# Decode attention over two KV caches: the V slots, the row length of A's V loads, and one softmax and one PV burst per K tile

## The chip, the cores and the metric

The kernel runs on one core of one Trainium2 chip. The core has five engines with instruction queues of their own: TensorE (PE), VectorE (DVE), ScalarE (ACT), GpSimd (POOL) and SyncE (SP). SP here does nothing but issue loads, in program order, on one load queue that 16 DMA engines work off. An engine waits for another through semaphores; an instruction that waits holds up all that stands behind it on its engine. The metric is the device time of one execution in microseconds (us): 830.06 is the median of three runs (829.58 to 830.49).

## The reference

Two independent attention blocks, A and B, each for a single query position, all in bf16:

```
q = x @ wq                      # x: 512 values, wq: 512 x 4096, 32 heads of 128
scores = q . k * 128**-0.5      # per head; every query head has its own K and V
p = softmax(scores)
o = p @ v                       # per head, 128 values
out = concat(o of 32 heads) @ wo   # wo: 4096 x 512
```

A attends to all 16384 positions of its cache, B to the last 4096 of its own. The result is A's 512 outputs followed by B's 512. K and V that must be read: A 32 heads x 16384 x 128 x 2 bytes twice, 268 MB; B 67 MB; the four weight matrices 16.8 MB; together 352 MB. There is one query per head, so every byte of K and V is used once.

## The kernel before, in words

**Tiles.** A "K tile" is 8 MB: 128 partitions with 256 positions of 128 values each. For A it holds a pair of heads (head h and 64 runs of 256 positions per head); for B two groups of four heads (4 heads x 32 runs of 128 positions per group, one group in each half of the tile). There are 20 K tiles, numbered T: 16 of A and 4 of B (T = 0, 7, 13 and 19). Each is worked on in two halves, u = 0 and 1, of `CH` = 128 positions per partition. To each K tile belongs a V tile of the same size and layout.

**Slots.** K tiles live in two slots of 64 KB per partition (`kring`). V lives in two slots of 32 KB per partition (`vring`), each a half V tile. The two wq matrices (4 MB each) start in the V slots. wo of A and the last half of V share the K slot that comes free at the end; wo of B takes a V slot.

**DVE: scores.** For each half tile: one product of K with q, 128x16384 (`scores_prod`, L194), four halving additions (`scores_tree`, L201), and a reduction to 128 scores per partition (L207). For A the two halves make one `Unit` (one softmax), for B each half is a unit of its own, with its own maximum.

**The softmax of a unit.** `unit_max` (L212, L214): DVE takes the maximum per partition, PE transposes it to one row. `max_all` (L219, L223, L226): DVE takes the maximum per head, spreads it, and PE turns it back into a column. `soft` (L231 to L242): ACT computes exp with its sum, and a masked copy of it per head (`pm`), so that heads in different partitions do not mix. `soft_sum` and `recip`: PE sums over partitions, DVE takes the reciprocal.

**PE: PV.** `pv` (L279) multiplies `pm` with V, four positions at a time: 32 matmuls of 128x512 per half V tile into one PSUM tile. `evict` (ACT, L295) scales it by the reciprocal, `columns` (PE L310, ACT L314) adds the four parts and turns it into columns of `O`. For the last K tile, `pv_columns` (L321) computes columns directly with 128 small matmuls per half.

**Order.** The whole program's order is written out by hand (`tc.manual_schedule()`): each engine runs its instructions in the order of these calls. In step T, u = 0, SP issues the first half of V(T-1), then K(T+1), and after the calls of PV the second half of V(T-1). The calls are:

```
            columns()
            scores_prod(T, u)
            if done is not None:
                max_all(done)
                soft(done)
                soft_sum(done)
            if u == 0 and T >= 1:
                if T >= 2:
                    pv(T - 2, 1)
                load_v(T - 1, 1)
                pv(T - 1, 0)
            nxt = scores_tree(T, u)
```

So one burst on PE is the second half of tile T-2 and the first half of tile T-1. A load is issued when the slot that it writes is free: K(T+1) when DVE is done with tile T-1, a V half when its slot's former PV is done.

**The end.** After the last K tile: the last softmax, the last PV half of tile 18, wo of B in five pieces (16, 8, 4, 2, 2 rows per partition, L145), `pv_columns` of the first half of tile 19, then for A `permute_o` (L331, L336), `project_out_columns` (L349, 128 small matmuls) and `store_out`; then `pv_columns` of the second half and the same three for B.

Of the kernel before, what the change touches and what calls it, by code (L numbers as in the profile page):

```python
# [25 lines left out]
def kernel(  # L26
# [26 lines left out]
    vring = ctx.enter_context(tc.tile_pool(name="vring", bufs=2))  # L53
# [10 lines left out]
    def vslot(name):  # L64
        return vring.tile([P, CH, DH], BF16, tag="vring", name=name)
# [58 lines left out]
    def load_v(T, u, dst=None):  # L124
        s, g = steps[T]
        V[T, u] = vslot("vt") if dst is None else dst
        if s is A:
            src = a_pair(A_v_cache, g)[:, u * CH : (u + 1) * CH, :].rearrange("p l d -> p (l d)")
        else:
            src = b_window(B_v_cache, 2 * g + u)  # L130
        nc.sync.dma_start(out=V[T, u][:, :, :].rearrange("p l d -> p (l d)"), in_=src)

    def load_wq(s):
        s.wq_t = vslot("wqt")
        nc.sync.dma_start(  # L135
            out=s.wq_t[:, :, :].rearrange("p a b -> p (a b)").rearrange("p (c f) -> p c f", c=KC),
            in_=s.wq.rearrange("(p c) f -> p c f", c=KC),
        )
# [24 lines left out]
    def project_q(s):  # L163
        wq = s.wq_t[:, :, :].rearrange("p a b -> p (a b)").rearrange(
            "p (c g h d) -> p c h g d", c=KC, h=s.nh, d=DH
        )
        for g in range(0, HQ // s.nh, 4):
            qp = ps_t.tile([P, 4, DH], F32, tag="tp", name="qp")
            n = KC * s.nh
            for k in range(n):  # L170
                c, j = divmod(k, s.nh)
                nc.tensor.matmul(  # L172
                    qp[:, :, :], lhsT=s.xb[:, j, c, :], rhs=wq[:, c, j, g : g + 4, :],
                    start=(k == 0), stop=(k == n - 1),
                )
            nc.scalar.copy(s.q[:, g : g + 4, :], qp[:, :, :])

    class Unit:
        def __init__(self, T, u):
            self.T = T  # L180
            self.s, g = steps[T]
            self.col = self.s.nh * g if self.s is A else self.s.nh * (2 * g + u)
            self.n = 2 * CH if self.s is A else CH
            self.rows = 4 * self.s.nh
            self.last = T == NT - 1
            self.sc = one.tile([P, 2 * CH], F32, tag="sc", name="sc")

# [8 lines left out]
    def scores_tree(T, u):  # L196
        s, g = steps[T]
        k = K[T][:, u * CH : (u + 1) * CH, :]
        w = DH // 2
        while w >= 8:  # L200
            nc.vector.tensor_tensor(out=k[:, :, 0:w], in0=k[:, :, 0:w], in1=k[:, :, w : 2 * w], op=ALU.add)  # L201
            w //= 2
        if s is B or u == 0:
            units[T, u] = Unit(T, u)
        un = units[T, u if s is B else 0]
        c0 = u * CH if s is A else 0
        nc.vector.tensor_reduce(out=un.sc[:, c0 : c0 + CH], in_=k[:, :, 0:8], axis=AX.X, op=ALU.add)  # L207
        return un if s is B or u == 1 else None

    def unit_max(un):  # L210
        m = small.tile([P, 1], F32, tag="m", name="m")
        nc.vector.tensor_reduce(out=m[:, :], in_=un.sc[:, 0 : un.n], axis=AX.X, op=ALU.max)  # L212
        un.sm = ps_m.tile([P, 512], F32, tag="sm", name="sm")
        nc.tensor.transpose(un.sm[0:1, 0:P], m[:, :], identf[:, :])  # L214

    def max_all(un):
        s = un.s
        M = small.tile([1, 4], F32, tag="M", name="M")
        nc.vector.tensor_reduce(  # L219
            out=M[:, 0 : s.nh], in_=by_head(s, un.sm[0:1, 0:P]), axis=AX.X, op=ALU.max  # L220
        )
        Mr = one.tile([1, P], F32, tag="Mr", name="Mr")
        nc.vector.tensor_copy(  # L223
            by_head(s, Mr[:, :]), M[:, 0 : s.nh].unsqueeze(2).broadcast_to([1, s.nh, P // s.nh])
        )
        nc.tensor.matmul(un.sm[:, 128:129], lhsT=Mr[:, :], rhs=one_f[:, :], start=True, stop=True)  # L226

    def soft(un):
        s = un.s
        bias = small.tile([P, 1], F32, tag="bias", name="bias")  # L230
        nc.scalar.activation(out=bias[:, :], in_=un.sm[:, 128:129], func=ACT.Copy, scale=-inv)  # L231
        p = one.tile([P, 2 * CH], BF16, tag="p", name="p")
        cs = small.tile([P, 1], F32, tag="cs", name="cs")
        nc.scalar.activation(  # L234
            out=p[:, 0 : un.n], in_=un.sc[:, 0 : un.n], func=ACT.Exp, scale=inv, bias=bias[:, :],
            accum_out=cs[:, :],
        )
        un.cs = cs
        pm = small.tile([P, 4 * CH], BF16, tag="pm", name="pm")
        un.pm = pm[:, 0 : un.n * s.nh].rearrange("p (i h c) -> p i h c", h=s.nh, c=4)  # L240
        for j in range(s.nh):
            nc.scalar.activation(  # L242
                out=un.pm[:, :, j, :], in_=p[:, 0 : un.n].rearrange("p (i c) -> p i c", c=4),
# [3 lines left out]
    def soft_sum(un):  # L247
        s, cs = un.s, un.cs
        if un.last:
            csm = small.tile([P, 4], F32, tag="csm", name="csm")  # L250
            nc.scalar.activation(out=csm[:, 0 : s.nh], in_=s.mask[:, :], func=ACT.Copy, scale=cs[:, :])
            nc.tensor.matmul(
                un.sm[:, 136 : 136 + s.nh], lhsT=ones_col[:, :].broadcast_to([P, P]), rhs=csm[:, 0 : s.nh],
                start=True, stop=True,
            )
        else:
            nc.tensor.matmul(  # L257
                un.sm[0 : un.rows, 136:137], lhsT=s.rows[:, :, :].rearrange("p a b -> p (a b)"), rhs=cs[:, :],
                start=True, stop=True,
            )  # L260

    def recip(un):
        un.r = small.tile([P, 4], F32, tag="r", name="r")
        if un.last:
            nc.vector.reciprocal(un.r[:, 0 : un.s.nh], un.sm[:, 136 : 136 + un.s.nh])
        else:
            nc.vector.reciprocal(un.r[0 : un.rows, 0:1], un.sm[0 : un.rows, 136:137])  # L267
# [3 lines left out]
    def pv(T, u):  # L271
        s = steps[T][0]
        un = units[T, u if s is B else 0]
        first, final = (True, True) if s is B else (u == 0, u == 1)
        if first:
            un.o = ps_o.tile([16, 512], F32, tag="o", name="o")
        i0 = u * CH // 4 if s is A else 0
        for i in range(CH // 4):
            nc.tensor.matmul(  # L279
                un.o[0 : un.rows, :],  # L280
                lhsT=un.pm[:, i0 + i, :, :].rearrange("p a b -> p (a b)"),
                rhs=V[T, u][:, 4 * i : 4 * i + 4, :],
                start=(first and i == 0),
                stop=(final and i == CH // 4 - 1),
            )
        if final:
            ready.append(un)
# [3 lines left out]
    def evict():  # L291
        while ready:
            un = ready.pop(0)
            un.osb = one.tile([16, 512], F32, tag="o4", name="o4")
            nc.scalar.activation(  # L295
                out=un.osb[0 : un.rows, :], in_=un.o[0 : un.rows, :], func=ACT.Copy,
                scale=un.r[0 : un.rows, 0:1],
            )
            evicted.append(un)
# [3 lines left out]
    def columns():  # L303
        while evicted:
            un = evicted.pop(0)
# [3 lines left out]
            for j in range(4):  # L309
                nc.tensor.matmul(  # L310
                    oc[:, 0 : s.nh], lhsT=un.osb[0:n, j * P : (j + 1) * P], rhs=sel[:, j, :],
                    start=(j == 0), stop=(j == 3),
                )
            nc.scalar.copy(s.O[:, un.col : un.col + s.nh], oc[:, 0 : s.nh])  # L314

    def pv_columns(T, u):
        un = units[T, u]
        s = un.s
        o = ps_o.tile([P, 4], F32, tag="o", name="ocol")
        for l in range(CH):  # L320
            nc.tensor.matmul(  # L321
                o[:, 0 : s.nh], lhsT=V[T, u][:, l, :], rhs=un.pm[:, l // 4, :, l % 4],
# [3 lines left out]
            out=s.O[:, un.col : un.col + s.nh], in0=o[:, 0 : s.nh], in1=un.r[:, 0 : s.nh], op=ALU.mult  # L326
# [51 lines left out]
    with tc.manual_schedule():  # L378
# [4 lines left out]
        load_wq(B)  # L383
        load_k(0, 0)
        load_wq(A)
# [17 lines left out]
        done = None  # L403
        for x in range(2 * NT):
            T, u = divmod(x, 2)
            if u == 0 and T >= 1:
                load_v(T - 1, 0)
# [3 lines left out]
            if x == 2 * NT - 2:  # L411
                W = kslot("wot")
                load_wo(A, W[:, 0:CH, :], (HQ,))
            if x == 2 * NT - 1:
                load_v(T, 0)
                load_v(T, 1, W[:, CH : 2 * CH, :])
            columns()
            scores_prod(T, u)
            if done is not None:
                max_all(done)  # L420
                soft(done)
                soft_sum(done)
            if u == 0 and T >= 1:
                if T >= 2:
                    pv(T - 2, 1)
                load_v(T - 1, 1)
                pv(T - 1, 0)
            nxt = scores_tree(T, u)
            if done is not None:
                recip(done)  # L430
            evict()
            done = nxt
            if done is not None:
                unit_max(done)
        columns()
        max_all(done)
        soft(done)
        pv(NT - 2, 1)
        load_wo(B, vslot("wot")[:, :, :], wo_pieces)
        soft_sum(done)  # L440
        recip(done)
        evict()
        pv_columns(NT - 1, 0)
        columns()
        permute_o(A)
        project_out_columns(A, (HQ,))
        store_out(A)
        pv_columns(NT - 1, 1)
# [33 lines left out]
```

## Time and profile before

| | |
|---|---|
| median of three runs | 830.06 us |
| the profiled execution's own time | 829.86 us |
| its span | 828.1 us |
| DVE busy | 761.4 us (92%) |
| PE busy | 387.3 us (47%) |
| ACT busy | 67.2 us (8%) |
| load queue of SP, share of the span of 16 DMA engines | 98.8% |
| read from HBM | 352.32 MB |
| last score of the last K tile (DVE, L207) ends | 791.4 us |
| last piece of B's wo is issued | 804.4 us |
| last output store is issued | 825.8 us |

The profile shows one execution, recorded by the hardware. A line of the timeline gives the start, the duration in us, the engine, the line of the program, the operation, what it writes and reads, the number of instructions merged into the line, and in brackets how long the engine sat idle before it and what ended that. "issue" means that nothing that the profile shows was waited for. A busy share is a mean over stages, and the slices (40 equal parts of the span) are read beside it: a digit of 9 is 90% or more. The granted clock of PE is 0.50 after idling, and 1.00 some microseconds into a burst.

### The profile page before, as it was taken

What the parts mean: (1) busy time and instruction counts of PE and PEld (TensorE: products, weight loads), DVE (VectorE), ACT (ScalarE), POOL (GpSimd) and SP (SyncE); (2) the same over time, 40 slices, a digit from 0 to 9 for tenths busy, and PEclk for the clock granted to TensorE, in tenths of its full rate; (3) what the DMA queues carried; (4) which work ended last, traced back from release to release, by engine and by line L of the source; (5) the groups of instructions that cost most, each with busy time, mean ns of one, the idle gap of its engine ahead of it and who ended that gap; (6) DMA issues with size and microseconds to landing.
All of it is one profiled execution on the core that took longest, in us unless ns stands there. A gap on an engine that the chain in (4) does not pass through costs nothing.

```text
span 828.1 us, 4994 instructions
## 1 busy us (share of the span) xinstructions
PE 387.3 (47%) x2100; PEld 171.3 (21%) x2100; DVE 761.4 (92%) x357; ACT 67.2 (8%) x195; POOL 0.7 (0%) x6
## 2 busy tenths in 40 slices
PE   3505061807173544637080826445362718081776
PEld 1201020303031212213030302122121203030335
DVE  1899999999999999999999999999999999999920
ACT  0111010101000001101010000011010101010110
POOL 0000000000000000000000000000000000000000
PEclk9766576859585868677685859586767767585975
DMA  9999999999999999999999999999999999999995
GB/s 380 431 431 431 428 453 423 449 416 436 431 427 431 431 440 423 439 423 455 412 450 416 452 412 432 442 423 445 419 443 418 441 421 444 424 432 432 430 430 240
DMA packets 10694, 352.64 MB, mean 426 GB/s; under 512 B 1456, under 2 KB 1456, under 8 KB 1840
## 3 DMA queue, kind: packets, MB, share of 16 engines
q1 hardware_dynamic: 10376, 352.33, 98.8%
q8 instruction: 16, 0.26, 0.1%
q10 hardware_dynamic: 296, 0.00, 0.0%
q14 instruction: 6, 0.05, 0.0%
HBM read 352.32 MB, written 0.00 MB: 425 GB/s over the span
## 4 chain that ended last, share of the span: by engine, by line
DVE 80%; DMA 15%; PE 3%; issue 1%; SPq 0%; ACT 0%; DVEq 0%
DVE kt L201 36%; DVE kt L194 36%; DMA kt<-in_A_k_cache_dram 10%; DVE sc L207 5%; DMA kt<-in_B_k_cache_dram 5%; PE o L279 1%; PE out_cols L349 1%; DVE m L212 1%; PE ocol L321 1%; DVE Mr L223 1%; DVE M L219 1%; DVE r L267 0%; SPq L135 0%; PE oc L310 0%; PE out_rows L367 0%
## 5 line engine op out<-in xcount | busy, mean ns | idle before, releaser
L201 DVE TENSOR_TENSOR kt<-kt 128x8192 bf16<-128x8192 bf16 (+3 forms) x160 | 344.9, 2156 | 4.7
L279 PE MATMUL o<-vt,pm 128*8 128x512 bf16 (+1 forms) x1216 | 306.7, 419 | 1.2 <-DMA vt<-in_A_v_cache_dram 1.2
L194 DVE TENSOR_TENSOR kt<-kt,qA 128x16384 bf16<-128x16384 bf16 x32 | 277.5, 8673 | 3.1 <-DMA kt<-in_A_k_cache_dram 3.1
L279 PEld LDWEIGHTS <-pm 128*8 128x8 bf16 (+1 forms) x1216 | 112.8, 94 | 185.4 <-issue 60.6
L214 PE MATMUL sm<-identf,m 128*1 128x128 f32 x24 | 8.5, 354 | 206.6 <-DVE m L212 206.6
L226 PE MATMUL sm<-one_f,Mr 1*128 1x1 f32 x48 | 13.3, 345 | 177.9 <-DVE Mr L223 177.9
L194 DVE TENSOR_TENSOR kt<-kt,qB 128x16384 bf16<-128x16384 bf16 x8 | 69.5, 8685 | 4.7 <-DMA kt<-in_B_k_cache_dram 4.7
L207 DVE TENSOR_REDUCE sc<-kt 128x128 f32<-128x1024 bf16 x40 | 48.8, 1220 | 2.9
L226 PEld LDWEIGHTS sm<-one_f,Mr 1*128 1x128 f32 x48 | 11.3, 291 | 184.8 <-DVE Mr L223 184.8
L214 PEld LDWEIGHTS sm<-identf,m 128*1 128x1 f32 x24 | 1.9, 79 | 209.6 <-issue 200.8
L231 ACT ACTIVATE bias<-sm 128x1 f32<-128x1 f32 x24 | 4.1, 171 | 399.5 <-PE sm L226 399.5
L295 ACT ACTIVATE o<-o,r 8x512 f32<-8x512 f32 (+1 forms) x22 | 14.9, 679 | 163.6 <-PE o L279 163.6
L310 PE MATMUL oc<-identf,o 8*128 8x2 f32 (+1 forms) x176 | 23.1, 249 | 2.4 <-ACT o L295 2.4
L310 PEld LDWEIGHTS oc<-identf,o 8*128 8x128 f32 (+1 forms) x176 | 21.2, 186 | 10.0 <-issue 6.5
L172 PE MATMUL qp<-wqt,scratch 128*128 128x512 bf16 x32 | 9.9, 486 | 13.5 <-DMA wqt<-in_B_wq_dram 13.5
L242 ACT ACTIVATE pm<-p,maskA 128x256 bf16<-128x256 bf16 x32 | 14.5, 501 | 0.5
L325 DVE TENSOR_TENSOR OB<-ocol,r 128x4 bf16<-128x4 f32 x2 | 0.3, 164 | 15.2 <-PE ocol L321 15.2
L172 PE MATMUL qp<-wqt,xbA 128*128 128x512 bf16 x32 | 8.7, 440 | 9.6 <-DMA wqt<-in_A_wq_dram 9.6
L314 ACT CAST OA<-oc 128x2 bf16<-128x2 f32 x16 | 2.6, 160 | 114.1 <-PE oc L310 114.1
L234 ACT ACTIVATE p<-sc,bias 128x256 bf16<-128x256 f32 (+1 forms) x24 | 11.3, 472 | 0.8
L242 ACT ACTIVATE pm<-p,maskB 128x128 bf16<-128x128 bf16 x32 | 10.2, 390 | 0.3
L257 PE MATMUL sm<-cs,rowsA 128*8 128x1 f32 x32 | 3.1, 167 | 14.3 <-ACT p L234 14.3
(59 smaller groups left out, 86.5 us busy)
## 6 DMA issues: line engine op xcount, KB each, us to landing
vt<-in_A_v_cache_dram SPq DMA_DIRECT2D x32, 4096.0 KB, 27.3
kt<-in_B_k_cache_dram SPq DMA_DIRECT2D x8, 4096.0 KB, 30.9
vt<-in_B_v_cache_dram SPq DMA_DIRECT2D x7, 4096.0 KB, 31.0
wqt<-in_B_wq_dram SPq DMA_DIRECT2D x1, 4096.0 KB, 12.8
wqt<-in_A_wq_dram SPq DMA_DIRECT2D x1, 4096.0 KB, 31.0
wot<-in_A_wo_dram SPq DMA_DIRECT2D x1, 4096.0 KB, 30.2
wot<-in_B_v_cache_dram SPq DMA_DIRECT2D x1, 4096.0 KB, 31.1
wot<-in_B_wo_dram SPq DMA_DIRECT2D x1, 2048.0 KB, 14.3
```

The costliest lines, as they stand in the source:

```text
L172: nc.tensor.matmul(qp[:, :, :], lhsT=s.xb[:, j, c, :], rhs=wq[:, c, j, g : g + 4, :], start=(k == 0), stop=(k == n - 1),)
L194: nc.vector.tensor_tensor(out=k, in0=k, in1=s.q[:, j : j + 1, :].broadcast_to([P, CH, DH]), op=ALU.mult)
L201: nc.vector.tensor_tensor(out=k[:, :, 0:w], in0=k[:, :, 0:w], in1=k[:, :, w : 2 * w], op=ALU.add)
L207: nc.vector.tensor_reduce(out=un.sc[:, c0 : c0 + CH], in_=k[:, :, 0:8], axis=AX.X, op=ALU.add)
L212: nc.vector.tensor_reduce(out=m[:, :], in_=un.sc[:, 0 : un.n], axis=AX.X, op=ALU.max)
L214: nc.tensor.transpose(un.sm[0:1, 0:P], m[:, :], identf[:, :])
L226: nc.tensor.matmul(un.sm[:, 128:129], lhsT=Mr[:, :], rhs=one_f[:, :], start=True, stop=True)
L234: nc.scalar.activation(out=p[:, 0 : un.n], in_=un.sc[:, 0 : un.n], func=ACT.Exp, scale=inv, bias=bias[:, :], accum_out=cs[:, :],)
L242: nc.scalar.activation(out=un.pm[:, :, j, :], in_=p[:, 0 : un.n].rearrange("p (i c) -> p i c", c=4), func=ACT.Copy, scale=s.mask[:, j : j ...
L279: nc.tensor.matmul(un.o[0 : un.rows, :], lhsT=un.pm[:, i0 + i, :, :].rearrange("p a b -> p (a b)"), rhs=V[T, u][:, 4 * i : 4 * i + 4, :], ...
L295: nc.scalar.activation(out=un.osb[0 : un.rows, :], in_=un.o[0 : un.rows, :], func=ACT.Copy, scale=un.r[0 : un.rows, 0:1],)
L310: nc.tensor.matmul(oc[:, 0 : s.nh], lhsT=un.osb[0:n, j * P : (j + 1) * P], rhs=sel[:, j, :], start=(j == 0), stop=(j == 3),)
```

## The change

- A's V tile is loaded in one transfer, with one row of 64 KB per partition, instead of two transfers with rows of 32 KB. B's V tile remains two transfers.
- `vring` has one slot of 64 KB per partition (a whole V tile) instead of two of 32 KB. V(T-1) is issued as a whole ahead of K(T+1).
- B's two units per tile become one with two parts: one maximum instruction over both, two transposes, one M and one Mr, two exp, one masked copy per head over both halves, one sum and one reciprocal.
- PV of a whole V tile is one burst of 64 matmuls in step T, after the softmax of tile T-1; for B two accumulations of 32.
- Both wq matrices share the one V slot at the start. At the end, wo of A and the first half of V(19) share the freed K slot; the second half of V(19), in two pieces, and wo of B share the V slot.
- For the last tile there is no maximum inside the loop; `permute_o(A)` comes before the last softmax, A's projection before the sums, and both `pv_columns` after it.

```diff
-    vring = ctx.enter_context(tc.tile_pool(name="vring", bufs=2))
+    vring = ctx.enter_context(tc.tile_pool(name="vring", bufs=1))
...
     def vslot(name):
-        return vring.tile([P, CH, DH], BF16, tag="vring", name=name)
+        return vring.tile([P, 2 * CH, DH], BF16, tag="vring", name=name)
...
+    def load_v(T):
         s, g = steps[T]
-        V[T, u] = vslot("vt") if dst is None else dst
+        V[T] = vslot("vt")
         if s is A:
-            src = a_pair(A_v_cache, g)[:, u * CH : (u + 1) * CH, :].rearrange("p l d -> p (l d)")
-        else:
-            src = b_window(B_v_cache, 2 * g + u)
-        nc.sync.dma_start(out=V[T, u][:, :, :].rearrange("p l d -> p (l d)"), in_=src)
+            nc.sync.dma_start(
+                out=V[T][:, :, :].rearrange("p l d -> p (l d)"),
+                in_=a_pair(A_v_cache, g).rearrange("p l d -> p (l d)"),
+            )
+        else:
+            for u in (0, 1):
+                load_v_half(T, u, V[T][:, u * CH : (u + 1) * CH, :])
+
+    def load_v_half(T, u, dst, pieces=1):
+        src = b_window(B_v_cache, 2 * steps[T][1] + u)
+        n = CH // pieces
+        for k in range(pieces):
+            nc.sync.dma_start(
+                out=dst[:, k * n : (k + 1) * n, :].rearrange("p l d -> p (l d)"),
+                in_=src[:, :, k * n * DH : (k + 1) * n * DH],
+            )
...
     def unit_max(un):
-        m = small.tile([P, 1], F32, tag="m", name="m")
-        nc.vector.tensor_reduce(out=m[:, :], in_=un.sc[:, 0 : un.n], axis=AX.X, op=ALU.max)
+        n = un.parts
+        m = small.tile([P, 2], F32, tag="m", name="m")
+        nc.vector.tensor_reduce(
+            out=m[:, 0:n], in_=un.sc[:, :].rearrange("p (v l) -> p v l", v=n), axis=AX.X, op=ALU.max
+        )
         un.sm = ps_m.tile([P, 512], F32, tag="sm", name="sm")
-        nc.tensor.transpose(un.sm[0:1, 0:P], m[:, :], identf[:, :])
+        for v in range(n):
+            nc.tensor.transpose(un.sm[0:1, v * P : (v + 1) * P], m[:, v : v + 1], identf[:, :])
...
+    def pv(un):
+        for v in range(un.parts):
+            o = ps_o.tile([16, 512], F32, tag="o", name="o")
+            m = un.n // 4
+            for i in range(m):
+                nc.tensor.matmul(
+                    o[0 : un.rows, :],
+                    lhsT=un.pm[:, v * m + i, :, :].rearrange("p a b -> p (a b)"),
+                    rhs=V[un.T][:, v * un.n + 4 * i : v * un.n + 4 * i + 4, :],
+                    start=(i == 0), stop=(i == m - 1),
+                )
+            ready.append((un, v, o))
...
-        for x in range(2 * NT):
-            T, u = divmod(x, 2)
-            if u == 0 and T >= 1:
-                load_v(T - 1, 0)
+        for T in range(NT):
+            if T >= 1:
+                load_v(T - 1)
                 if T + 1 < NT:
                     new_k(T + 1)
                     load_k(T + 1)
-            if x == 2 * NT - 2:
+            if T == NT - 1:
                 W = kslot("wot")
                 load_wo(A, W[:, 0:CH, :], (HQ,))
-            if x == 2 * NT - 1:
-                load_v(T, 0)
-                load_v(T, 1, W[:, CH : 2 * CH, :])
+                load_v_half(T, 0, W[:, CH : 2 * CH, :])
             columns()
...
+            scores_prod(T, 0)
+            if T >= 1:
+                max_all(units[T - 1])
+                soft(units[T - 1])
+                soft_sum(units[T - 1])
+                pv(units[T - 1])
+            scores_tree(T, 0)
+            if T >= 1:
+                recip(units[T - 1])
+            scores_prod(T, 1)
+            scores_tree(T, 1)
             evict()
+            if T < NT - 1:
+                unit_max(units[T])
+        Z = vslot("wot")
+        load_v_half(NT - 1, 1, Z[:, 0:CH, :], 2)
+        load_wo(B, Z[:, CH : 2 * CH, :], wo_pieces)
+        un = units[NT - 1]
         columns()
         permute_o(A)
+        unit_max(un)
+        max_all(un)
+        soft(un)
         project_out_columns(A, (HQ,))
+        soft_sum(un)
+        recip(un)
+        pv_columns(un, 0, W[:, CH : 2 * CH, :])
         store_out(A)
-        pv_columns(NT - 1, 1)
+        pv_columns(un, 1, Z[:, 0:CH, :])
         permute_o(B)
         project_out_columns(B, wo_pieces)
         store_out(B)
```

## The prediction

> **What bounds the kernel now.** I read the engine totals first, then the slices, then the places where VectorE (DVE) waits, then TensorE's bursts, then the tail in order of time.
>
> ```profile
> span 828.1 us, 4994 instructions
> ...
> PE 387.3 (47%) x2100; PEld 171.3 (21%) x2100; DVE 761.4 (92%) x357; ACT 67.2 (8%) x195; POOL 0.7 (0%) x6
> ...
> DMA  9999999999999999999999999999999999999995
> ...
> q1 hardware_dynamic: 10376, 352.33, 98.8%
> ```
>
> DVE looks like the bound with 92%, but SP's load queue is occupied for 98.8% of the span. Which of the two sets the pace is seen where DVE starts a K tile:
>
> ```profile
> 598.26 8.69 DVE L194 TENSOR_TENSOR kt<-kt,qA 128x16384 bf16<-128x16384 bf16 x1 [1.23 <-DMA kt<-in_A_k_cache_dram]
> ...
> 637.04 8.69 DVE L194 TENSOR_TENSOR kt<-kt,qA 128x16384 bf16<-128x16384 bf16 x1 [0.54 <-DMA kt<-in_A_k_cache_dram]
> ...
> 676.05 8.69 DVE L194 TENSOR_TENSOR kt<-kt,qA 128x16384 bf16<-128x16384 bf16 x1 [0.79 <-DMA kt<-in_A_k_cache_dram]
> ...
> 714.84 8.69 DVE L194 TENSOR_TENSOR kt<-kt,qA 128x16384 bf16<-128x16384 bf16 x1 [0.56 <-DMA kt<-in_A_k_cache_dram]
> ```
>
> From 598 us on, every K tile lands after DVE is ready for it. The steps are 38.78, 39.01 and 38.79 us, mean 38.86, for 16.78 MB (one K tile and one V tile): 431.7 GB/s. The slices show the same rate from the second one on; earlier, DVE (38.13 us per tile) merely used up a lead that the loads had. So the end is: all bytes at 432 GB/s, done at about 821.8 us (the last piece of B's wo is issued at 804.4 and lands 17.4 us later), and then a tail of 6.3 us. Only a higher rate, a hole in the stream of loads, or the tail can move the time.
>
> The bursts of probabilities times V (PV), 64 matmuls each, matter because the change makes V loads wait for them:
>
> ```profile
> 149.01 15.69 PE L279 MATMUL o<-vt,pm 128*8 128x512 bf16 x64
> ...
> 187.14 15.40 PE L279 MATMUL o<-vt,pm 128*8 128x512 bf16 x64
> ...
> 225.28 16.79 PE L279 MATMUL o<-vt,pm 128*8 128x512 bf16 x64
> ...
> 656.71 7.07 PE L279 MATMUL o<-vt,pm 128*8 128x512 bf16 x32 [0.37 <-DMA vt<-in_A_v_cache_dram]
> ```
>
> A warm half takes 7.07 us (221 ns a matmul), so 64 would take 14.1. A burst that starts cold (granted clock 0.50 for the first microseconds, then 1.00) takes 15.4 to 16.8 us, depending on when the clock is raised.
>
> The tail, PE alone:
>
> ```profile
> 812.57 1.17 PE L321 MATMUL ocol<-pm,wot 128*128 128x4 bf16 x37
> 815.81 2.57 PE L321 MATMUL ocol<-pm,wot 128*128 128x4 bf16 x91 [2.07 <-issue]
> ...
> 819.80 0.99 PE L349 MATMUL out_cols<-OpB,wot 128*128 128x1 bf16 x32 [0.27 <-ACT OpB L340]
> 822.01 2.70 PE L349 MATMUL out_cols<-OpB,wot 128*128 128x1 bf16 x96 [1.21 <-issue]
> ```
>
> Two stalls have no data behind them ("issue"). Counting matmuls and weight loads between them gives 256 instructions; 256 further back lies a seam at 809.58, with no stall. So PE's instructions come in blocks of 256, and a block is ready some 6.2 us after the one before it was entered: 809.58 to 815.81 and 815.81 to 822.01. The seam before, at about 804.15, was followed after 5.4 us without a stall. I call this time F, 5.4 to 6.2 us.
>
> **The change part by part.** All against the profiled execution: span 828.1, time 829.86, which is 0.2 under the median 830.06.
>
> *Rows of 64 KB.* Same bytes. With 32 KB rows alone (from wq B's landing at 13.53 to the second half of B's first K tile at 42.68) 12.58 MB took 29.15 us, 431.6 GB/s; with half of the bytes in 64 KB rows it is 431.7. I take 0. The three steps above differ by 0.23 us at most; half of that over 16 tiles bounds this part by 1.9 us either way.
>
> *One V slot.* Before, the queue always held work: V halves were issued about 7 us apart as each half's PV ended. Now V(T) may be issued only when the whole PV(T-1) has ended, and PV(T-1) starts only when all of V(T-1) has landed. Behind V on SP's queue stands K(T+2); it needs DVE's end of tile T, which comes later anyway. While PV(T-1) runs, K(T+1) fills the queue: 19.43 us. The ring from V landing to V landing is PV (P) + about 0.1 us of semaphores + a load's fixed cost + 19.43; without a hole it may last 38.86. The only load issued to an empty queue is wq B: issued at 0.74, landed at 13.53, of which 4.19 MB take 9.71, so 3.08 us are fixed. The ring is closed without a hole if P is below 38.86 - 19.43 - 3.08 - 0.1 = 16.25. Taking P evenly spread from 15.1 to 16.8, the mean excess is 0.55 x 0.55 / (2 x 1.7) = 0.09 us. Sixteen loads wait for such a burst (behind B's tiles the first half lands and runs early): 1.4 us. Bounds: 0 if the fixed cost in mid-run is 2.5 us or less; and if it grows by the time of the larger row (32 KB at 27 GB/s per engine are 1.2 us) the limit is 15.05, the mean excess 0.90 and the sum 14.4 us. I take 1.4: the measured fixed cost is of the same queue and size class, and K's 64 KB tiles do not land later than their bytes explain.
>
> Here a rule speaks against the change: the Trainium skill ("Trainium Kernel Development and Optimization", Best Practices) says to double-buffer so that loads overlap with compute. If the V slot's emptying stood alone in the queue, that rule would cost 16 us for each of 16 tiles, 256 us in all; the trace's 19.43 us of K beside each burst is why I do not use that sum.
>
> *One softmax per B tile.* Removes on DVE four times a max (0.29), an M (0.27), an Mr (0.23) and a reciprocal (0.15): 3.8 us. It lies under the loads (38.13 against 38.86 us per tile), so it is worth 0; were DVE the bound again it would be worth up to 3.8. ACT makes four masked copies of 0.50 instead of eight of 0.39, PE two transposes in a row: under DVE's first product of the tile. SP issues 16 V loads fewer (0.33 us each), hidden by its waits.
>
> *Order of the loads and the tail.* K(T+1) now stands behind all of V(T-1), not half: every K tile from the second on lands 9.72 us later, while the last byte stays at 821.8. So K tile 18 lands at 724.5 and DVE finishes tile 19 at 800.4 instead of 791.4. PV(18) starts with V(18)'s landing (four halves before the end, 782.9), ends at 798.9; its columns and the permutation end at 801.8; the two transposes, M, Mr and two matmuls at 804.2 let A's projection start. From there PE needs four instruction blocks. In the built order the seams fall after matmul 50 of A's projection (805.6), 49 of the first column PV, 48 of the second and 43 of B's projection. With F the three later seams come no sooner than 805.6 + F, + 2F, + 3F: the last at 821.8 (F 5.4) to 824.2 (F 6.2), then 85 matmuls of 28 ns, 2.4: PE ends at 824.2 to 826.6, where it now ends at 824.7. So -0.5 to +1.9; with F at 5.8, +0.7, and I take +0.9, since two of three readings are 6.2. If F no longer limits, PE ends when the last 8 matmuls follow the last landing, 822.0: -2.7. That is the lower bound of this part.
>
> On this the Trainium skill ("Runtime: NRT & Kernel Launch", Instruction fetch mechanics) says instructions are refilled in blocks of 256 and that PE's store holds 2048, so that fetching stays hidden. The block size agrees with the 256 counted above; the hiding does not, with stalls of 2.07 and 1.21 us. By the page this part would be -2.7, by the rows +0.9.
>
> Sum: 0 + 1.4 + 0 + 0.9 = +2.3, so 832.2 in this execution's terms and 832.4 beside the median.
>
> **The rivals.** *Not slower, faster (the other side):* the tail's instruction blocks arrive in time. For it: V's last half now comes in two pieces, so PE starts on it earlier, and wo pieces have small rows that may let the fetches through. Against it: the second stall was as long as the first although the loads were then of smaller rows. Without holes it gives 829.86 - 2.7 = 827.2, with the row gain 825.3. It decides when F is under about 5 us. *Nothing moves:* no holes (P is below the limit in 11 of the 16 unbroken bursts of 64) and F near 5.4 to 5.6: 829.4 to 830.9. *Holes in every tile:* the fixed cost is higher for 64 KB rows; 829.86 + 14.4 + 0.9 = 845.2, and 835 to 845 in between. For it: no row shows a load into an empty queue in mid-run. Against it: K tiles landing on time.
>
> **How the numbers follow.** Forecast (831 to 835): 0.40. Faster: 0.20. Nothing: 0.20. Holes in every tile: 0.20. A measurement of this kernel (829.58 to 830.49) can tell about 0.2% from no change, 1.7 us: under 828.4 is faster (0.20), over 831.7 slower (0.20 and 0.35 of the forecast's 0.40: 0.55), the rest 0.25. The range leaves a tenth out on each side: 827 to 842.
>
> **What would show it.** In the changed profile, DMA's slices stay at 9 and 431 GB/s; if SP's wait for PV ends later than 17 us after V's landing, or K tiles are further apart than 38.9 us, there are holes. DVE should wait for K in every tile by about 0.7 us, and end near 800. PE should show "issue" stalls in both column PVs and B's projection, about 6 us apart. I am wrong if the steps between K tiles shrink (64 KB rows are faster), if they grow by more than a microsecond, or if the stalls are gone.

## The result, and the profile after

The changed kernel takes 843.13 us (median of four runs, 840.53 to 843.78) against 830.01 for the kernel before: ratio 1.0151, 95% interval [1.0139, 1.0163]. It is slower by 13.1 us, as forecast in sign, and far more than the 2.4 us that I gave as the likeliest; the range ended at 842.

The page of the changed kernel, profiled at 843.26 us:

```profile
span 841.5 us, 4924 instructions
...
PE 389.9 (46%) x2092; PEld 178.1 (21%) x2092; DVE 761.3 (90%) x341; ACT 62.5 (7%) x175; POOL 0.7 (0%) x6
...
DMA  9999999999999999999999999999999999999996
...
q1 hardware_dynamic: 8216, 352.33, 97.9%
...
DMA 54%; DVE 30%; PE 14%; issue 1%; ACT 1%; SPq 0%; DVEq 0%
DMA kt<-in_A_k_cache_dram 34%; DMA vt<-in_A_v_cache_dram 15%; DVE kt L209 14%; DVE kt L215 13%; PE o L310 11%; DMA kt<-in_B_k_cache_dram 5%; DVE sc L219 2%; PE out_cols L378 1%; PE ocol L349 1%; DVE M L244 0%; PE sm L250 0%; ACT pm L271 0%; DVE Mr L248 0%; SPq L147 0%; DVE Mr L246 0%
```

DVE and PE do as much as before, the bytes are the same. The slices of the loads still read 9 nearly everywhere: a hole of one or two microseconds does not show in a slice of 21. What does show is the chain that ended last (the last two lines): PV (`PE o L310`) now stands on it with 11% and V's loads with 15%; in the kernel before the chain was

```profile
DVE 80%; DMA 15%; PE 3%; issue 1%; SPq 0%; ACT 0%; DVEq 0%
```

The places are seen where DVE starts K tiles, on DVE's timeline of the changed kernel:

```profile
141.31 8.69 DVE L209 TENSOR_TENSOR kt<-kt,qA 128x16384 bf16<-128x16384 bf16 x1 [0.49 <-DMA kt<-in_A_k_cache_dram]
...
181.90 8.69 DVE L209 TENSOR_TENSOR kt<-kt,qA 128x16384 bf16<-128x16384 bf16 x1 [2.36 <-DMA kt<-in_A_k_cache_dram]
...
220.95 8.69 DVE L209 TENSOR_TENSOR kt<-kt,qA 128x16384 bf16<-128x16384 bf16 x1 [0.82 <-DMA kt<-in_A_k_cache_dram]
...
261.41 8.69 DVE L209 TENSOR_TENSOR kt<-kt,qA 128x16384 bf16<-128x16384 bf16 x1 [2.24 <-DMA kt<-in_A_k_cache_dram]
```

The steps are 40.59, 39.05 and 40.46 us; the bytes need 38.8. K tile 18 starts at 734.68, 10.2 us later than the 724.5 of the prediction. The loads and bursts between these starts, first SP's timeline, then PE's:

```profile
138.68 0.33 SPq L128 DMA_DIRECT2D vt<-in_A_v_cache_dram  x1
...
177.49 0.33 SPq L128 DMA_DIRECT2D vt<-in_A_v_cache_dram  x1
...
217.59 0.33 SPq L128 DMA_DIRECT2D vt<-in_A_v_cache_dram  x1
```

```profile
162.02 15.44 PE L310 MATMUL o<-vt,pm 128*8 128x512 bf16 x64 [9.86 <-DMA vt<-in_A_v_cache_dram]
...
201.29 16.27 PE L310 MATMUL o<-vt,pm 128*8 128x512 bf16 x64 [8.53 <-DMA vt<-in_A_v_cache_dram]
...
241.75 16.52 PE L310 MATMUL o<-vt,pm 128*8 128x512 bf16 x64 [9.94 <-DMA vt<-in_A_v_cache_dram]
```

One turn of the ring can be read off. V lands at 162.02, the burst ends at 177.46, 0.03 us later the next V load is issued (177.49), K lands at 181.90, V at 201.29. In the turn before, V was issued at 138.68, K landed at 141.31 and V at 162.02, 20.71 us after K, although 8.39 MB take 19.4: a hole of 1.3 us. The turn after it (issue 217.59, K at 220.95, V at 241.75) has one of 1.4 us. In these three turns V's loads were issued only 2.6 to 4.4 us ahead of the landing of the K tile in front of them.

The tail, PE's timeline again:

```profile
816.74 3.57 PE L378 MATMUL out_cols<-OpA,wot 128*128 128x1 bf16 x128
...
823.34 2.28 PE L349 MATMUL ocol<-pm,wot 128*128 128x4 bf16 x80 [1.32 <-issue]
...
829.54 2.30 PE L349 MATMUL ocol<-pm,wot 128*128 128x4 bf16 x81 [2.45 <-issue]
...
835.73 2.43 PE L378 MATMUL out_cols<-OpB,wot 128*128 128x1 bf16 x86 [1.21 <-issue]
```

Three stalls without a releaser, 6.20 and 6.19 us apart, after 48, 47 and 42 small matmuls (128 less the 80, 81 and 86 that follow). This part went as worked out.

The last V tile of A lands at 795.10 where the prediction's timeline without holes had 782.9: 12.2 us of holes. The rest of the 13.4 us between the spans, 1.2, is the tail.

### The profile page after: what moved, and what is told of

The parts are those of the page before. It is cut to its first block, busy times and chain, and to the rows that moved or that the text cites. A ratio compares the mean times of both kernels' runs of the same rounds, so it can differ in the third digit from the quotient of the medians.

```text
span 841.5 us, 4924 instructions
## 1 busy us (share of the span) xinstructions
PE 389.9 (46%) x2092; PEld 178.1 (21%) x2092; DVE 761.3 (90%) x341; ACT 62.5 (7%) x175; POOL 0.7 (0%) x6
## 4 chain that ended last, share of the span: by engine, by line
DMA 54%; DVE 30%; PE 14%; issue 1%; ACT 1%; SPq 0%; DVEq 0%
DMA kt<-in_A_k_cache_dram 34%; DMA vt<-in_A_v_cache_dram 15%; DVE kt L209 14%; DVE kt L215 13%; PE o L310 11%; DMA kt<-in_B_k_cache_dram 5%; DVE sc L219 2%; PE out_cols L378 1%; PE ocol L349 1%; DVE M L244 0%; PE sm L250 0%; ACT pm L271 0%; DVE Mr L248 0%; SPq L147 0%; DVE Mr L246 0%
## 5 line engine op out<-in xcount | busy, mean ns | idle before, releaser
L310 PE MATMUL o<-vt,pm 128*8 128x512 bf16 (+1 forms) x1216 | 304.0, 417 | 153.6 <-DMA vt<-in_A_v_cache_dram 149.0
L310 PEld LDWEIGHTS <-pm 128*8 128x8 bf16 (+1 forms) x1216 | 113.5, 94 | 336.2 <-issue 191.2
L231 PE MATMUL sm<-identf,m 128*1 128x128 f32 x24 | 6.7, 312 | 79.2 <-DVE m L226 79.2
L339 PE MATMUL oc<-identf,o 8*128 8x2 f32 (+1 forms) x176 | 28.3, 279 | 0.8 <-ACT o L324 0.8
L339 PEld LDWEIGHTS oc<-identf,o 8*128 8x128 f32 (+1 forms) x176 | 26.4, 226 | 5.9 <-issue 2.7
L258 ACT ACTIVATE bias<-sm 128x1 f32<-128x1 f32 (+1 forms) x20 | 3.4, 171 | 196.6 <-PE sm L250 196.6
L184 PE MATMUL qp<-wqt,xbA 128*128 128x512 bf16 x32 | 9.7, 477 | 10.2 <-DMA wqt<-in_A_wq_dram 10.2
L244 DVE TENSOR_REDUCE M<-sm 1x2 f32<-1x128 f32 (+1 forms) x20 | 6.0, 299 | 3.9 <-PE sm L231 3.9
```

Source lines behind the costliest of these rows:

```text
L184: nc.tensor.matmul(qp[:, :, :], lhsT=s.xb[:, j, c, :], rhs=wq[:, c, j, g : g + 4, :], start=(k == 0), stop=(k == n - 1),)
L310: nc.tensor.matmul(o[0 : un.rows, :], lhsT=un.pm[:, v * m + i, :, :].rearrange("p a b -> p (a b)"), rhs=V[un.T][:, v * un.n + 4 * i : v * ...
L339: nc.tensor.matmul(oc[:, 0 : s.nh], lhsT=osb[0:n, j * P : (j + 1) * P], rhs=sel[:, j, :], start=(j == 0), stop=(j == 3),)
```

## The experiments

Two theories to begin with. "Ring": V landing, PV burst, issue of the next V, its landing is longer than the bytes allow. "Rows": 64 KB rows make V's loads slower. Each edit is against the changed kernel unless said otherwise.

**e1: V in 32 KB rows, PV still after all of V**

```diff
+            for u in (0, 1):
+                nc.sync.dma_start(
+                    out=V[T][:, u * CH : (u + 1) * CH, :].rearrange("p l d -> p (l d)"),
+                    in_=a_pair(A_v_cache, g)[:, u * CH : (u + 1) * CH, :].rearrange("p l d -> p (l d)"),
+                )
...
-            for i in range(m):
+            order = [(i + m // 2) % m for i in range(m)] if un.s is A else list(range(m))
+            for k, i in enumerate(order):
...
-                    start=(i == 0), stop=(i == m - 1),
+                    start=(k == 0), stop=(k == len(order) - 1),
```

> A's V tile goes in two loads of 32 KB rows into the same single slot, and PV starts with the second half, so that the burst still waits for the whole V tile. Theory 'ring' (V landing, PV burst, issue of the next V load, its landing: longer than the 38.86 us that the bytes need, because a load's fixed cost in mid-run is some 4 us and not 3.08; row length plays no part): as the changed kernel, 840 to 845 us, holes of 10 to 14 us in all. Theory 'rows' (64 KB rows make the V load itself or its fixed cost slower): holes fall to a few us, 831 to 835 us.

845.01 us, ratio 1.0177 [1.0155, 1.0199]. As slow as with 64 KB rows: the row length is not the cause.

**e2: the same loads, PV in natural order**

> As the run before, but PV in its natural order: the burst may start when the first half of V has landed, 9.7 us before the second. One slot, one softmax and the new tail stay. Ring: the slot comes free some 8 us earlier, the queue never runs dry, holes 0 to 1 us; what is left of the change is the tail, +1.2 us: 830 to 832.5 us. Rows: the same 830 to 833, since the rows are 32 KB here too; this run tells apart only together with the run before.

829.84 us, ratio 0.9995 [0.9986, 1.0005]: no difference from the kernel before. Only the order of matmuls within the burst differs from e1, and 15 us are gone. K tiles start 38.8 us apart through most of the run, and K tile 18 starts at 724.61, where the prediction without holes had 724.5. On DVE's timeline:

```profile
179.99 8.69 DVE L210 TENSOR_TENSOR kt<-kt,qA 128x16384 bf16<-128x16384 bf16 x1 [0.56 <-DMA kt<-in_A_k_cache_dram]
...
218.79 8.69 DVE L210 TENSOR_TENSOR kt<-kt,qA 128x16384 bf16<-128x16384 bf16 x1 [0.57 <-DMA kt<-in_A_k_cache_dram]
```

**e3: half the burst**

```diff
-            for i in range(m):
+            order = list(range(m // 2)) if un.s is A else list(range(m))
+            for k, i in enumerate(order):
...
-                    start=(i == 0), stop=(i == m - 1),
+                    start=(k == 0), stop=(k == len(order) - 1),
```

> The changed kernel with 64 KB rows, but PV of A's tiles computes only the first 32 of its 64 matmuls (the other half of the positions is left out of A's output); all loads stay. Ring: the burst is 8.6 us instead of 16, the next V load is issued 7 us earlier, holes gone: 830 to 833 us, K tiles 38.9 us apart. Rows: unchanged, 840 to 845 us.

828.11 us (one run), below the 830 to 833 that the ring was given, with the single slot and the 64 KB rows unchanged. DVE's timeline of this run:

```profile
140.64 8.69 DVE L209 TENSOR_TENSOR kt<-kt,qA 128x16384 bf16<-128x16384 bf16 x1 [0.48 <-DMA kt<-in_A_k_cache_dram]
...
179.42 8.69 DVE L209 TENSOR_TENSOR kt<-kt,qA 128x16384 bf16<-128x16384 bf16 x1 [0.55 <-DMA kt<-in_A_k_cache_dram]
...
218.12 8.69 DVE L209 TENSOR_TENSOR kt<-kt,qA 128x16384 bf16<-128x16384 bf16 x1 [0.47 <-DMA kt<-in_A_k_cache_dram]
...
256.83 8.69 DVE L209 TENSOR_TENSOR kt<-kt,qA 128x16384 bf16<-128x16384 bf16 x1 [0.49 <-DMA kt<-in_A_k_cache_dram]
```

The steps are 38.78, 38.70 and 38.71 us. With the burst out of the way the loads run without holes.

**e4: a longer burst**

```diff
-            for i in range(m):
+            order = list(range(m)) + list(range(8)) if un.s is A else list(range(m))
+            for k, i in enumerate(order):
...
-                    start=(i == 0), stop=(i == m - 1),
+                    start=(k == 0), stop=(k == len(order) - 1),
```

> The changed kernel with 8 matmuls more in each of A's PV bursts (8 of the 64 are added a second time, so that A's output is another), 1.77 us per burst. Ring: nearly every ring is at its limit, so 16 of them grow by 1.3 to 1.8 us each: 864 to 872 us. Rows: PE has over 15 us of idle time per tile, so nothing changes, 840 to 845 us.

863.38 us (one run), 20.3 above the changed kernel and just under the interval given. PE idles for over 15 us per tile, yet 1.77 us more of it per burst cost some three quarters of that on each of 16 turns. e3 and e4 together show that the burst's length sets the pace.

**e5: a warm burst**

```diff
+                if steps[T - 1][0] is A:
+                    dum = ps_t.tile([P, 4, DH], F32, tag="tp", name="dum")
+                    for _ in range(24):
+                        nc.tensor.matmul(dum[:, :, :], lhsT=ident[:, :], rhs=A.q[:, 0:4, :], start=True, stop=True)
                 pv(units[T - 1])
```

> The changed kernel with 24 matmuls on TensorE, results unused, between the softmax of an A tile and its PV burst, in the 8.5 us that TensorE idles there; the burst then starts with the clock up and takes 14.2 to 14.6 us instead of 15.4 to 16.7. Ring: with the fixed cost of 2.3 to 5.0 us seen in the runs before, the ring is 36 to 39 us, so holes of 0 to 2 us are left of 12: 829 to 832 us. Any theory in which the single slot costs something other than the burst's length: 840 to 845 us.

830.12 us, ratio 1.0001 [0.9992, 1.001]: useless work takes away the whole loss. The bursts on PE's timeline:

```profile
160.36 13.97 PE L310 MATMUL o<-vt,pm 128*8 128x512 bf16 x64 [1.89 <-DMA vt<-in_A_v_cache_dram]
...
199.07 13.97 PE L310 MATMUL o<-vt,pm 128*8 128x512 bf16 x64 [0.77 <-DMA vt<-in_A_v_cache_dram]
```

14 of A's 16 bursts take 13.97 us instead of 15.3 to 16.7; the two that follow a wait of 2.17 and 2.54 us take 15.66. Two microseconds of slack on a ring are worth 13 us of the kernel.

**e6: row length alone**, in the kernel before, whose queue never drains: A's K tiles in two loads of 32 KB rows.

```diff
-            nc.sync.dma_start(
-                out=K[T][:, :, :].rearrange("p l d -> p (l d)"),
-                in_=a_pair(A_k_cache, g).rearrange("p l d -> p (l d)"),
-            )
+            for v in (0, 1):
+                nc.sync.dma_start(
+                    out=K[T][:, v * CH : (v + 1) * CH, :].rearrange("p l d -> p (l d)"),
+                    in_=a_pair(A_k_cache, g)[:, v * CH : (v + 1) * CH, :].rearrange("p l d -> p (l d)"),
+                )
```

> The kernel before, with A's K tiles too in two loads of 32 KB rows instead of one of 64 KB rows; the queue is never empty there, so row length acts alone. Row length is nothing (the prediction's term of 0): 830.2 +- 0.3 us. Rows of 64 KB are slightly faster (as the steps between K tiles hint, 38.71 us in the run with the half PV against 38.79 in the run with V in 32 KB rows): 0.08 us per tile for 16 tiles, 831.2 to 832 us.

831.18 us, ratio 1.0012 [1.0003, 1.0021]. Two issues instead of one 64 KB load per tile cost 1.2 us over 16 tiles, 0.07 us each. So 64 KB rows, loaded at once, are a small gain.

**e7: a better version.** e2, with A's projection moved ahead of the last softmax, where PE idles.

```diff
         permute_o(A)
+        project_out_columns(A, (HQ,))
         unit_max(un)
         max_all(un)
         soft(un)
-        project_out_columns(A, (HQ,))
         soft_sum(un)
```

> V in two loads of 32 KB rows with PV in natural order (829.84 us) and, besides, A's output projection ahead of the last softmax on TensorE's queue, where it idles for 7 us. If blocks of 256 instructions 6.2 us apart set the end, the chain of seams starts some 8 us earlier, the stalls fall before the last bytes land, and the end follows the last piece of B's wo: 2.5 us less, 826.8 to 827.8 us. If the seams are not the limit: 829.5 to 830.2.

827.83 us, ratio 0.9973 [0.9962, 0.9983]: faster than both kernels. The last stall on PE's timeline:

```profile
814.19 2.30 PE L350 MATMUL ocol<-pm,wot 128*128 128x4 bf16 x81 [1.98 <-issue]
...
820.39 2.43 PE L379 MATMUL out_cols<-OpB,wot 128*128 128x1 bf16 x86 [1.21 <-issue]
```

It ends at 820.39 instead of 822.01 in the kernel before. Two stalls remain, 6.20 us apart, so the end still follows the blocks and not the last bytes; hence 2.2 us and not 2.7.

**e8: the warm burst and the moved projection together**, the same edit on e5.

> Run with the warm burst and A's projection moved forward: V in 64 KB rows, no holes, no seams at the end. With 64 KB rows worth 0.08 us per tile: 825 to 827.5 us; if holes remain, 828 to 831.

830.31 us, ratio 1.0007 [0.9997, 1.0016]: no gain, and in the interval given for holes that remain. Some do: K tile 18 starts at 725.43, 1.0 us later than in e7. Besides, PV of tile 18 begins only when all of V(18) has landed and ends at 799.2, not 789.8 as in e7. PE then is not idle where the projection was put: the last transposes start at 805.68 instead of 800.63 in e5, behind the moved projection:

```profile
783.58 15.66 PE L310 MATMUL o<-vt,pm 128*8 128x512 bf16 x64 [2.47 <-DMA vt<-in_A_v_cache_dram]
...
802.40 3.42 PE L378 MATMUL out_cols<-OpA,wot 128*128 128x1 bf16 x128 [0.27 <-ACT OpA L369]
805.68 0.59 PE L231 MATMUL sm<-identf,m 128*1 128x128 f32 x2
```

How much each of the two costs was not separated. The version with both gains was not found.

**e9 and e10: a load by itself.** 24 more matmuls per burst, so that K has landed before the next V load is issued; with V in 64 KB rows and, on e1's loads, in 32 KB rows.

```diff
-            for i in range(m):
+            order = list(range(m)) + list(range(24)) if un.s is A else list(range(m))
+            for k, i in enumerate(order):
...
-                    start=(i == 0), stop=(i == m - 1),
+                    start=(k == 0), stop=(k == len(order) - 1),
```

> The changed kernel with 24 matmuls more in each of A's PV bursts (24 of the 64 are added a second time, so that A's output is another), 21.3 us in all: now K has landed about 2 us before the next V load is issued, and every V load meets an empty queue. Issue to landing, less 19.4 us for 8.39 MB, is then the fixed cost by itself. If it is the constant 3.08 us of the prediction: V lands 22.5 us after its issue each time, K tiles 43.8 us apart, some 910 us. If it is 2.3 to 5.0 us, mean 3.7, as the run with 8 more matmuls hints: 22 to 24.5 us, 918 to 924 us.

> The same 24 extra matmuls with A's V in two loads of 32 KB rows, PV starting with the second half. If rows of 64 KB raise the fixed cost (one packet of 64 KB takes an engine 2.4 us, one of 32 KB 1.2 us), issue to landing is shorter and less spread here by about 1 us, and the time some 15 us under the 64 KB run. If row length plays no part: within 4 us of it.

905.49 and 903.07 us (one run each). SP's and PE's timelines of e9:

```profile
143.32 0.33 SPq L128 DMA_DIRECT2D vt<-in_A_v_cache_dram  x1
...
185.72 0.33 SPq L128 DMA_DIRECT2D vt<-in_A_v_cache_dram  x1
```

```profile
165.20 20.49 PE L311 MATMUL o<-vt,pm 128*8 128x512 bf16 x88 [13.55 <-DMA vt<-in_A_v_cache_dram]
...
207.67 21.43 PE L311 MATMUL o<-vt,pm 128*8 128x512 bf16 x88 [12.29 <-DMA vt<-in_A_v_cache_dram]
```

Issue to landing is 21.88 and 21.95 us, less 19.43 for the bytes 2.45 and 2.52. Of 13 such loads, 11 lie between 2.27 and 2.69 (the others 3.1 and 3.8); with 32 KB rows 11 of 13 lie between 2.23 and 2.38. Both expectations of e9 failed: the fixed cost into an empty queue is neither 3.08 nor 2.3 to 5.0, it is about 2.4. e10 lies 2.4 us from e9, as was expected if row length plays no part. In e4, where K landed mostly 1.6 to 2.4 us after V was issued (0.7 and 3.5 in two of 13 loads), the same difference was 2.3 to 5.0, in two groups around 2.4 and 4.8. SP's and PE's timelines of e4:

```profile
179.72 0.33 SPq L128 DMA_DIRECT2D vt<-in_A_v_cache_dram  x1
...
221.46 0.33 SPq L128 DMA_DIRECT2D vt<-in_A_v_cache_dram  x1
```

```profile
204.13 17.30 PE L311 MATMUL o<-vt,pm 128*8 128x512 bf16 x72 [11.94 <-DMA vt<-in_A_v_cache_dram]
...
243.28 18.20 PE L311 MATMUL o<-vt,pm 128*8 128x512 bf16 x72 [8.59 <-DMA vt<-in_A_v_cache_dram]
```

From issue to landing these two loads took 24.41 and 21.82 us. K landed 1.61 and 2.38 us after the issue. By e9's 21.9 us, the first load would have landed within half a microsecond of the same time if it had been issued 2.2 us later, into the empty queue (an estimate).

**The last of sixteen engines.** The kept traces hold more than the views above print: a load has 16 completions, as many as there are DMA engines, and what waits for the load goes on after the last. In both groups of e4 the median of the 16 came 21.4 to 21.9 us after the issue. The groups differ by the last, which was 0.2 to 0.8 us behind the median in one and 2.3 to 2.8 in the other (one load of the 13 is an exception: its median came after 23.5 us). In e9 it is 0.2 to 0.6 us behind, except in the two outliers, 1.0 and 1.5. A fetch of instructions (a packet of 8 or 16 KB, on queues of their own) fell into each of these two, and in seven of e9's K loads the last engine was 1.5 to 1.9 us behind with such a fetch of 16 KB, about 1 us long, in them. In the changed kernel's 13 V loads that wait for one of A's bursts the median comes 2.0 to 3.2 us after issue beyond the bytes (mean 2.4) and the last engine 0.9 to 2.7 us after that (mean 1.7). So when V was issued, the last engine was still 2.6 to 4.4 us from landing its part of K, but the median one only 0.2 to 3.1.

**e11 and e12: is it the packets still in flight?** A's K tiles in four loads of 16 KB rows, V unchanged; then K and V so, with PV starting at V's last quarter.

```diff
-            nc.sync.dma_start(
-                out=K[T][:, :, :].rearrange("p l d -> p (l d)"),
-                in_=a_pair(A_k_cache, g).rearrange("p l d -> p (l d)"),
-            )
+            for w in range(4):
+                c = slice(w * CH // 2, (w + 1) * CH // 2)
+                nc.sync.dma_start(
+                    out=K[T][:, c, :].rearrange("p l d -> p (l d)"),
+                    in_=a_pair(A_k_cache, g)[:, c, :].rearrange("p l d -> p (l d)"),
+                )
```

> The changed kernel with A's K tiles in four loads of 16 KB rows; V stays in rows of 64 KB. Into an empty queue a V load has a fixed cost of 2.4 us, yet a V load that joins the last 2 to 4 us of a K tile lands up to 2.5 us later than either that or the K tile's end would make it. Theory 'packet': the packets still in flight when V is issued (64 KB, 2.4 us on one engine) are what delays it; with 16 KB (0.6 us) the holes fall from 12 us to under 4, 833 to 836 us, plus 1 to 3 us for the shorter rows. Theory 'not the packets of K': 842 to 848 us.

> A's K and V in four loads of 16 KB rows each, PV starting with the last quarter of V, so that the burst still waits for the whole V tile. Packet theory, whether K's or V's packets count: 834 to 839 us. Otherwise 843 to 850 us, as much as the run with V in 32 KB rows or more.

847.0 us, ratio 1.0206 [1.0161, 1.025], and 846.75, ratio 1.0203 [1.0173, 1.0232]. The size of the packets is not it; the theory falls, and both times lie in the intervals given for that.

## Why the prediction was right or wrong

- *What bounds the kernel: right.* The bytes at some 432 GB/s set the pace. Wherever the queue stayed filled (e2, e3), the K tiles came mostly 38.7 to 38.8 us apart, and DVE then waited for each by half a microsecond.
- *The V slot's ring: the right mechanism, far too small, and this is the step that failed.* I gave 1.4 us, the runs 12. The failing sentence is that the ring is closed without a hole if the burst is below 16.25 us, with a fixed cost of 3.08 taken from the first load of the program. The burst was as forecast (15.3 to 16.7). A constant was the wrong form: into an empty queue the cost is smaller than I took, 2.4 us (with that alone there would be no holes at all), but a load that joins a queue with a few microseconds left can lose up to 2.5 us more, and mostly on the last of the 16 engines alone. In the first load of the program that engine was 0.2 us behind the median. In the changed kernel, issue to landing less the bytes is 3.1 to 5.2 us over the 13 loads that wait for one of A's bursts, mean 4.1 (2.4 for the median engine, 1.7 more for the last), and with it the ring is 16.0 + 0.03 + 4.1 + 19.4 = 39.5 us; from V landing to V landing those 13 turns took 38.7 to 41.0 us, mean 39.56. At 0.7 us over the 38.86 of the prediction they make 9.1 of the 12.2 us; the rest was lost around B's tiles 7 and 13, where two turns took 80.0 and 78.8 us. I had the form that this takes among the rivals, "holes in every tile" with 14.4 us, but for a wrong reason: the larger row. e1, e11 and e12 show no part of the row length in it.
- *The rows: taken as 0, within the bound of 1.9.* 1.2 us for 16 tiles (e6). For V it was not run by itself, but K's steps of 38.70 us in e3 against 38.79 in e2 agree, and so do the completions: behind a full queue a V tile in 64 KB rows (e3) lands 19.34 to 19.37 us after the load ahead of it, and the first half of one in 32 KB rows (e2) 9.70 to 9.73.
- *The softmax on DVE: right that it is worth 0, wrong in its size.* Its 16 instructions fewer show nowhere on the chain. But the 3.8 us counted only what goes: the instructions over both halves take longer (M 407 ns instead of 273), so that maxima, M, Mr and reciprocals together take 22.1 us instead of 24.8; DVE's busy time in all is the same to 0.1 us.
- *The tail: right in place and size.* Expected +0.9, found 1.2. The stalls fell after 48, 47 and 42 matmuls, where 49, 48 and 43 were given, and 6.20 us apart, the upper end of F. In the other runs with two or more stalls they end 5.4 to 6.5 us apart. The Trainium skill ("Runtime: NRT & Kernel Launch", Instruction fetch mechanics) has the blocks of 256 right; that the cost of crossing into the next one is mostly hidden, as it says, was not so in any of these tails. The rival "the blocks arrive in time" was wrong: PE stalled two or three times in the tail of every run, once in e8's, and e7 gained 2.2 us by starting the chain of blocks earlier, not by faster blocks.
- *Why the loss is this steep.* The burst starts cold every time: PE idled 8.5 us and more before each of A's bursts, the granted clock was 0.50 at its start (for 3 us in the burst at 162.02), and filling that gap (e5) made the burst 13.97 us. The Trainium skill ("TensorE: Matmul & The Clock Gate", HAM oscillation) says that TensorE must not idle for more than about 3.4 us if its clock is to stay up; here less was enough, for in e5 it fell to 0.50 after waits of 2.17 and 2.54 us, though not after 1.93. I saw the cold start in the profile, priced it into the burst's range, and did not ask what the rest of the ring would bear.

**Open:** why one engine is late with a load that joins a queue which is about to drain. It is not V's rows, nor the packets of K in front of it. Fetches of instructions set single engines back in e9, but no run took them away, and none fell into the load of e4 issued at 179.72, whose last engine was 2.8 us behind the median.

## What to carry to other kernels

When loads set the pace, ask of every slot how much work is still queued when its next load is issued, and want several microseconds more than the fixed cost of a load into an empty queue. With 3 us left the loads lost up to 2 us each; with 5.3 us and more left (e5) one of twelve lost 0.9 us and the others 0.2 or nothing; with 10 us left, after B's tiles and in e2, none did. A ring through another engine (landing, compute, issue, landing) is priced turn by turn with the last of the DMA engines, not with a mean, and its compute started cold here (granted clock 0.50) wherever nothing filled the gap.

## What the runs showed of the hardware that I had not expected

- A load of 8.39 MB into an empty queue costs 2.4 us beyond its bytes, with little spread; one issued 1.6 to 2.4 us before the queue drains may cost 2.5 us more than that (e4, e9). Most of the difference is the last of 16 engines: the median one lands 2.0 to 2.5 us beyond the bytes in 12 of e4's 13 such loads and 2.0 to 2.2 in all of e9's.
- 64 KB rows against two loads of 32 KB rows: 1.2 us on 134 MB (e6), a tenth of a percent of the kernel.
- A block of 256 PE instructions took 6.2 us to arrive in the tails of the kernel before, the changed kernel and e7, whether the loads beside it moved in packets of 16 KB (the first block of the changed kernel's tail) or of 8 KB and less (the third). In the kernel before, the fetches are seen as packets of 16 KB that start at 807.08, 813.30 and 819.44; PE goes on 2.5 us after each.
